# A fused attention and gated-FFN layer on one core: remainder weight rows in three loads, a slack on the q/k weights, and the last token block in two column pieces

## The chip, the cores and the metric

The kernel runs on one core of one Trainium2 chip. The metric is the device time of one execution in microseconds (us), the median of several. The core has a matrix engine (TensorE, PE in the profile), a vector engine (DVE), an activation engine (ScalarE, ACT), GpSimd (POOL) and SyncE (SP). Most DMAs are issued by SP, in program order; the scatter of q and k within SBUF is issued by POOL. Each engine runs its own instruction list in order, and waits on semaphores for the others.

## The reference

`x` has 2048 tokens of 576 features. It is layer-normalized; one branch is causal attention with 32 heads of 18 features and a window of 256 tokens, the other a gated FFN of width 4608. The result is `x` plus their gated product:

```python
xn = layernorm(x)
s  = attention(xn, wqkv, window=256) @ wo          # 32 heads of 18
h  = sigmoid(xn @ w_gate) * (xn @ w_up)            # 576 -> 4608
g  = silu(h @ w_down)                              # 4608 -> 576
return x + s * g                                   # bfloat16
```

## The kernel before

**Stages.** The tokens are taken in four stages of 512 (four blocks of 128). Each stage has a layernorm with transposes, v for its four blocks, five groups of q/k columns (128 columns each; the fifth is the rest of both), attention by eight groups of four heads, the product with wo, and the FFN: gate and up for 36 tiles of 128 hidden columns (`gate_up`, L828), the gating (`tail`, L844) and the down product (`down`, L885), last the gated sum and the store of each block (`build_final`, L909).

**Contraction of 576 as 64 + 4 x 128.** The 576 input features do not divide by 128. The first 64 weight rows, the *remainder rows*, have a tensor of their own, and the other 512 stand as four layers of 128 partitions. `load_nat` (L391) loads the 512, `load_rem` (L395) the 64. `pair` (L89) issues two matmuls of 64 rows each, one on each half of the array, and `turn` (L97) makes one *half* of a product: half 0 has ten matmuls and begins with the remainder rows, half 1 has eight and finishes the sum. So a product of gate and up of one tile is f10 (half 0, ten matmuls) and f11 (half 1, eight), and likewise qk0 and qk1, v0 and v1. For gate/up, the upper and lower partition halves of the remainder tensor `wgr` hold gate rows and up rows.

**Weights.** Gate and up are loaded in *groups* of two tiles, 256 KB from each of the two matrices, into a ring of four slots `wgs` (`weights`, L804); each of the four stages loads them again. The remainder rows of gate and up stay in `wgr` for all stages. Before the change they come in two loads of each matrix, set by `REM` (L57): the one beside group 0 covers groups 0 to 3, the one beside group 2 covers groups 4 to 17. A gate/up half of stage 0 waits for the loads of its own group and for those of the span that holds it. The q/k weights are `wqk` (two loads of 576 KB) and `wqkr` (two of 72 KB), those of v are `wv_sb` (576 KB) and `wvr` (two of 36 KB) (L423 to L426). The five copies L427 and L431 make the fifth q/k group's weights from `wqk` and `wqkr`.

**The order of the work is made by a planner.** The code first writes a graph of operations, each with an engine, an estimated duration, a priority (a smaller number goes first) and dependencies. `schedule` (L948) then goes through it as a list scheduler: at each step the operation that can start first by its own estimates is put at the end of its engine's list. A DMA is taken to end 2.5 us after its issue, or later if the bytes ahead of it need longer; a field `slack` adds to that end (used before the change for the loads of x, L387). `emit` writes the lists as they are, with waits on semaphores. So an estimate is no wait, it only moves places: on the chip each engine keeps its order, and an operation whose data is late holds up everything behind it on its engine.

**The start.** SP issues four loads of x, then group 0 and the first remainder span, groups 1 and 2, the second remainder span, group 3, the q/k weights, the v weights, then group 4 and so on. PE warms up on zeros (`NWARM`), transposes the normalized x, and does gate/up of tiles 0 to 2 (in two token halves each), then of tiles 3 and 4 except for the second half of tile 4. Behind that stand four halves of q/k, then v mixed with gate/up of tiles 4 to 6, then the first scores.

**The end.** The last stage's `build_final` differs from the others': ACT makes the tanh of each half of the columns, DVE multiplies the attention result with the PSUM value (L933, two halves of 288 columns), then combines (L938) and adds x (L943), and one DMA stores the block. The 576 output columns of a block lie in two PSUM banks of 288 (`halves`, L520); `down` does 36 hidden tiles in two turns over the partition halves, 72 pairs of matmuls of 288 columns.

Of the kernel before, what the change touches and what calls it, by code (L numbers as in the profile page):

```python
# [8 lines left out]
D = 576  # L9
# [79 lines left out]
def pair(eng, outs, lhs, rhs, start, stop, swap=0):  # L89
    res = None  # L90
    for i in range(2):
        t = i ^ swap
        res = eng.matmul(outs[i], lhs(ROWS[t], i), rhs(ROWS[t], i), start=start, stop=stop, tile_position=(64 * t, 0))  # L93
    return res
# [125 lines left out]
class Builder:  # L220
# [566 lines left out]
    def build_ffn(self, c):  # L787
# [16 lines left out]
        def weights(wg):  # L804
            sw, dw = self.r_w.produce()
            pr = 1 + wg if c == 0 and wg < 4 else 3
            fc = slice(wg * WG * P, (wg + 1) * WG * P)
            ds = [self.load_nat(self.wgs[:, sw, :, i, :], w[:, fc], f"dma:w:{c}:{wg}", ("w", sw, i), pr, [dw])
                  for i, w in enumerate((self.wg, self.wu))]
            if c == 0 and wg in REM:  # L810
                f8 = slice(REM[wg][0] * WG * P, REM[wg][1] * WG * P)
                self.op_wgr[wg] = self.load_rem(self.wgr[:, f8], (self.wg[:, f8], self.wu[:, f8]), f"dma:wgr:{wg}", ("wgr", wg), pr)
            if c == 0:
                ds += self.op_wgr[0 if wg < 4 else 2]
            slots[wg] = sw
            wops[wg] = ds

# [64 lines left out]

        new_last = [None] * NFG

        def down(i, h, swap, deps):  # L885
            cols = slice(i * P, (i + 1) * P)
            for q in range(NFG):
                def f(eng, q=q):
                    res = None
                    for ft in range(q * FG, (q + 1) * FG):  # L890
                        res = pair(eng, self.halves(h, 288), lambda r, t: self.hT[r, ft, cols],
                                   lambda r, t: self.wd_sb[r, ft, 288 * t:288 * t + 288],
                                   swap == 0 and ft == 0, swap == 1 and ft == NFT - 1, swap)
                    return res
                o = pe(FG * mm_ns(288), f, f"f2:{c * BPC + i}:{swap}:{q}",
                       [[hm[ft] for ft in range(q * FG, (q + 1) * FG)], self.op_wd[q], deps],
                       h if q == 0 and swap == 0 else None)
# [11 lines left out]
    def build_final(self, sb, h, f2):  # L909
        op = self.op  # L910
        sx, dx = self.r_xf.produce()
        st, dt_ = self.r_th.produce()
        rows = slice(sb * P, (sb + 1) * P)
        o_dx = self.dma(self.xf[:, sx, :], self.x[rows, :], P * D * 2, f"dma:xf:{sb}", ("xf", sx), deps=[dx, self.hm[8]], prio=6)
        t, xf, s_ = self.thf[:, st, :], self.xf[:, sx, :], self.s_attn[:, sb % BPC, :]

        def y2():
            return self.both(h, 288)

        def v2(a):  # L920
            return a.rearrange("p (t c) -> p t c", t=2)
        def f_th(e, a, b):
            return e.activation(v2(t)[:, a:b, :], y2()[:, a:b, :], ACTF.Tanh, scale=0.25)  # L923
        if sb < (NC - 1) * BPC:
            th = op("ACT", act_ns(D), lambda e: f_th(e, 0, 2), f"fth:{sb}", deps=[f2, dt_], prio=0)
            q1 = op("DVE", dve_ns(D), lambda e: e.scalar_tensor_tensor(v2(t), v2(t), 1.0, y2(), ALU.add, ALU.mult),  # L926
                    f"fq1:{sb}", deps=[th, f2], prio=0)
            q2 = op("DVE", dve_ns(D, 2.0), lambda e: e.tensor_tensor(t, t, s_, ALU.mult), f"fq2:{sb}",
                    deps=[q1, self.op_s[sb]], prio=2)
            h.release(q1)  # L930
        else:
            def f_w(e, a):
                return e.tensor_tensor(v2(s_)[:, a, :], v2(s_)[:, a, :], y2()[:, a, :], ALU.mult)  # L933
            th0 = op("ACT", act_ns(D // 2), lambda e: f_th(e, 0, 1), f"fth:{sb}:0", deps=[f2, dt_], prio=0)
            w1 = op("DVE", dve_ns(D // 2), lambda e: f_w(e, 1), f"fq1:{sb}:1", deps=[f2, self.op_s[sb]], prio=0)
            th1 = op("ACT", act_ns(D // 2), lambda e: f_th(e, 1, 2), f"fth:{sb}:1", deps=[w1, dt_], prio=0)
            w0 = op("DVE", dve_ns(D // 2), lambda e: f_w(e, 0), f"fq1:{sb}:0", deps=[th0, w1], prio=0)
            q2 = op("DVE", dve_ns(D), lambda e: e.scalar_tensor_tensor(t, t, 1.0, s_, ALU.add, ALU.mult), f"fq2:{sb}",  # L938
                    deps=[w0, th0, th1], prio=0)
            h.release(w0)  # L940
            h.release(th1)
        self.op_q2[sb] = q2
        q3 = op("DVE", dve_ns(D, 2.0), lambda e: e.tensor_tensor(xf, xf, t, ALU.add), f"fq3:{sb}", deps=[q2, o_dx], prio=2)  # L943
        self.r_th.release(st, q3)
        o = self.dma(self.out[rows, :], xf, P * D * 2, f"dma:out:{sb}", ("out", sx), deps=[q3], prio=2)
        self.r_xf.release(sx, o)

    def schedule(self):  # L948
        ENGS = ("PE", "ACT", "DVE", "POOL", "SP")
# [196 lines left out]
```

## Time and profile before

| | us |
|---|---|
| median of five runs | 593.98 (593.0 to 594.95) |
| the profiled execution | 594.95 |
| its span, from first to last instruction | 593.2 |
| PE busy | 575.6 |
| DVE busy | 345.8 |
| ACT busy | 274.5 |
| POOL busy | 176.3 |
| first gate/up matmul | 10.08 |
| first q/k matmul | 24.48 |
| first v matmul | 32.13 |
| first scores | 40.43 |
| last matmul ended | 588.20 |
| last DVE instruction ended | 590.50 |

Times inside the profile count from the start of the span. A line of the timeline has the start, the length, the engine, the source line, the operation with its output and input, and in brackets how long the engine sat idle before it and what released it. Matmuls are pipelined: the length of a merged line is what counts, not the mean of one. Where a line holds a DMA issue (SPq, POOLq), the length is that of issuing; the landing is given separately as the time from issue to landing. The two halves of a pair count as two matmuls.

### The profile page before, as it was taken

Reading aid. Unit: us, or ns where it says so; the run is one execution under the profiler, and the core shown is the slowest. Engines: PE = TensorE matmul, PEld = TensorE weight load, DVE = VectorE, ACT = ScalarE, POOL = GpSimd, SP = SyncE. Lnnn points to the kernel's source line nnn. Section 1 sums busy time; section 2 is a strip of 40 time slices with the busy share of each in tenths; the row PEclk is TensorE's granted clock in tenths of the full one; section 3 lists DMA queues with packets and bytes.
Section 4 is the critical chain, followed back from the end, with each engine's and each line's share of the span. In section 5 each row is a group of like instructions: output and inputs, shape, how many; then the busy total and the mean of one; then the engine's idle time right before and its main releaser. Section 6 shows DMA issues by size and latency. Waiting matters only on the chain.

```text
span 593.2 us, 21412 instructions
## 1 busy us (share of the span) xinstructions
PE 575.6 (97%) x9528; PEld 359.4 (61%) x9528; DVE 345.8 (58%) x837; ACT 274.5 (46%) x389; POOL 176.3 (30%) x286
## 2 busy tenths in 40 slices
PE   8798999999999999999999999999999999999996
PEld 7364455567788556455587775555447764444775
DVE  4268888855978783687866378867431133333122
ACT  2145667545556744587764356765230123233111
POOL 5362755108463440454620644340000000000000
PEclk9799999999999999999999999999999999999998
DMA  8936654642111442344300213333351113542010
GB/s 225 280 106 206 192 162 133 195 132 59 47 34 50 111 115 67 104 116 122 101 22 29 51 31 98 99 114 107 111 152 30 38 56 112 160 142 73 2 42 21
DMA packets 95724, 60.09 MB, mean 101 GB/s; under 512 B 7020, under 2 KB 94012, under 8 KB 95632
## 3 DMA queue, kind: packets, MB, share of 16 engines
q1 hardware_dynamic: 90512, 53.98, 31.9%
q0 software_dynamic: 5120, 4.74, 3.2%
q8 instruction: 75, 1.23, 0.9%
q14 instruction: 17, 0.14, 0.1%
HBM read 51.61 MB, written 2.36 MB: 91 GB/s over the span
## 4 chain that ended last, share of the span: by engine, by line
PE 83%; DVE 5%; DMA 3%; POOL 3%; SPq 3%; issue 2%; ACT 1%; DVEq 0%; POOLq 0%
PE ps L93 82%; POOL qk L249 3%; SPq L249 3%; DMA qk<-qd 2%; DVE qd L550 1%; DVE hT L849 1%; DMA wqkr<-in_A_wqkv_dram 1%; DVE pvs L728 1%; ACT tring L846 1%; PE ps L512 1%; DVE kx L627 1%; DVE v_aug L610 0%; ACT expr L662 0%; DVE expr L675 0%; DVE s_attn L933 0%
## 5 line engine op out<-in xcount | busy, mean ns | idle before, releaser
L93 PE MATMUL ps<-xnT,wgs 64*128 64x512 bf16 (+1 forms) x2352 | 287.2, 372 | 0.1
L662 ACT ACTIVATE expr<-ps 128x1024 bf16<-128x1024 f32 (+2 forms) x160 | 153.3, 983 | 63.0 <-PE ps L93 62.3
L93 PEld LDWEIGHTS ps<-xnT,wgs 64*128 64x128 bf16 x2352 | 112.6, 94 | 111.4 <-PE ps L93 0.9
L93 PE MATMUL ps<-wd_sb,hT 64*128 64x288 bf16 x2304 | 155.5, 283 | 0.0
L846 ACT ACTIVATE tring<-ps 128x512 bf16<-128x512 f32 x144 | 85.7, 598 | 135.7 <-PE ps L93 133.4
L849 DVE SCALAR_TENSOR_TENSOR hT<-tring,ps 128x512 bf16<-128x512 bf16 x144 | 98.1, 684 | 79.2 <-ACT tring L846 75.9
L93 PEld LDWEIGHTS ps<-wd_sb,hT 64*128 64x128 bf16 x2304 | 111.8, 94 | 27.9
L249 POOL DMA_DIRECT2D qk<-qd x160 | 81.8, 520 | 112.6 <-DVE qd L550 77.5
L675 DVE TENSOR_TENSOR expr<-expr,mask 128x256 bf16<-128x256 bf16 (+2 forms) x232 | 65.7, 307 | 39.8 <-ACT expr L662 38.7
L627 POOL TENSOR_SCALAR kx<-kprev,small 128x256 bf16<-128x256 bf16 x64 | 63.9, 1006 | 73.3 <-PE ps L93 73.0
L93 PE MATMUL ps<-xnT,wgr 64*128 64x512 bf16 (+1 forms) x294 | 55.5, 373 | 5.0 <-DVE hT L849 3.3
L93 PE MATMUL ps<-qk,kx 64*128 64x320 bf16 (+4 forms) x736 | 57.5, 251 | 0.7 <-DVE qd L550 0.3
L728 DVE TENSOR_REDUCE pvs<-ps 64x304 f32<-64x608 f32 x64 | 50.4, 787 | 8.6 <-PE ps L93 7.1
L93 PEld LDWEIGHTS ps<-qk,kx 64*128 64x128 bf16 x736 | 31.4, 94 | 23.8 <-DVE qd L550 1.2
L93 PEld LDWEIGHTS ps<-v_aug,expr 64*128 64x128 bf16 x2432 | 35.3, 93 | 7.4 <-DVE expr L675 2.2
L923 ACT ACTIVATE thf<-ps 128x576 bf16<-128x576 f32 (+1 forms) x20 | 11.1, 555 | 61.7 <-PE ps L93 61.4
L93 PE MATMUL ps<-v_aug,expr 64*128 64x19 bf16 (+1 forms) x2432 | 35.9, 170 | 0.9 <-DVE expr L675 0.8
L93 PE MATMUL ps<-xnT,wqk 64*128 64x512 bf16 x256 | 35.1, 399 | 0.0
L627 DVE TENSOR_SCALAR kx<-qk,small 128x512 bf16<-128x512 bf16 x64 | 23.6, 393 | 10.2 <-DMA qk<-qd 9.8
L550 DVE CAST qd<-ps 128x1024 bf16<-128x1024 f32 (+1 forms) x20 | 22.2, 1115 | 9.2 <-PE ps L93 8.9
L93 PEld LDWEIGHTS ps<-xnT,wgr 64*128 64x128 bf16 x294 | 14.6, 94 | 20.4 <-DVE hT L849 6.1
L926 DVE SCALAR_TENSOR_TENSOR thf<-thf,ps 128x576 bf16<-128x576 bf16 x12 | 9.0, 753 | 29.6 <-ACT thf L923 29.4
(65 smaller groups left out, 306.8 us busy)
## 6 DMA issues: line engine op xcount, KB each, us to landing
wgs<-in_B_w_gate_dram SPq DMA_DIRECT2D x72, 256.0 KB, 3.1
wgs<-in_B_w_up_dram SPq DMA_DIRECT2D x72, 256.0 KB, 3.5
wd_sb<-in_B_w_down_dram SPq DMA_DIRECT2D x9, 576.0 KB, 4.1
qk<-qd POOLq DMA_DIRECT2D x100, 36.0 KB, 1.9
xf<-in_A_x_dram SPq DMA_DIRECT2D x16, 144.0 KB, 2.3
out_dram<-xf SPq DMA_DIRECT2D x16, 144.0 KB, 1.8
xr<-in_A_x_dram SPq DMA_DIRECT2D x6, 288.0 KB, 3.3
wqk<-in_A_wqkv_dram SPq DMA_DIRECT2D x2, 576.0 KB, 11.0
```

Source lines behind the costliest of these rows:

```text
L93: res = eng.matmul(outs[i], lhs(ROWS[t], i), rhs(ROWS[t], i), start=start, stop=stop, tile_position=(64 * t, 0))
L249: o = self.op(eng, DMA_ISSUE_NS[eng], lambda e: e.dma_start(dst, src), name, deps, prio, nbytes=nbytes)
L512: res = eng.transpose(self.psb[:, o:o + 64], src(r, k * P), self.ident[r, :], tile_position=(64 * t, 0))
L550: return eng.tensor_copy(dst, self.both(h, n))
L627: return e.tensor_scalar(self.kx[:, sx, pos:pos + n_ // SW, t, :], src.rearrange("p (s k) -> p s k", k=SW), self.half[:, t:t + 1], None, A ...
L662: return eng.activation(self.expr[:, se, :, lo * SW:NT], self.both(h, NT)[:, :, lo * SW:NT], ACTF.Exp, scale=SM_SCALE)
L675: return eng.tensor_tensor(e_, e_, m_, ALU.mult)
L728: return eng.tensor_reduce(out[ROWS[i]], src, mybir.AxisListType.X, ALU.add)
L846: th = op("ACT", act_ns(NT), lambda e: e.activation(self.tring[:, st, :], bank(h, 0), ACTF.Tanh, scale=0.5), f"th:{c}:{ft}", deps=[pg, dt_ ...
L849: mu = op("DVE", dve_ns(NT), lambda e: e.scalar_tensor_tensor(self.hT[:, ft, :], self.tring[:, st, :], 1.0, bank(h, 1), ALU.add, ALU.mult) ...
L923: return e.activation(v2(t)[:, a:b, :], y2()[:, a:b, :], ACTF.Tanh, scale=0.25)
L926: q1 = op("DVE", dve_ns(D), lambda e: e.scalar_tensor_tensor(v2(t), v2(t), 1.0, y2(), ALU.add, ALU.mult), f"fq1:{sb}", deps=[th, f2], prio=0)
```

## The change

Three things are edited.

1. `REM` has three spans in place of two, each with a priority of its own: groups 0 and 1 beside group 0 (priority 1), groups 2 to 5 beside group 2 (priority 3), groups 6 to 17 beside group 3 (priority 7). Each span is a load from gate and one from up: 2 x 64 KB, 2 x 128 KB and 2 x 384 KB, in place of 2 x 128 KB and 2 x 448 KB. The group that needs a span waits for it.
2. The four loads of the q/k weights get a slack of 2500 ns in the planner.
3. In the last stage's last two blocks, the down product of block 15 is made in two column pieces: columns 0 to 383 (192 in each bank) and 384 to 575 (96 in each bank, `NTAIL`), the second one in a further PSUM hold from the attention's pool. On PE the first half of the small piece stands ahead of the last of the nine groups of hidden tiles of the large one (`NFG - 1`), and its second half comes last. `build_final` runs once for each piece; the store of the block stays one DMA and waits for both.

```diff
+NTAIL = 96
...
-REM = {0: (0, 4), 2: (4, 18)}
+REM = {0: (0, 2, 1), 2: (2, 6, 3), 3: (6, 18, 7)}
...
         self.op_wqk += self.load_rem(self.wqkr[:, :], (wq, wk), "dma:wqkr", ("wqkr",), 5)
+        for o in self.op_wqk:
+            o.slack = 2500.0
...
-                self.op_wgr[wg] = self.load_rem(self.wgr[:, f8], (self.wg[:, f8], self.wu[:, f8]), f"dma:wgr:{wg}", ("wgr", wg), pr)
+                self.op_wgr[wg] = self.load_rem(self.wgr[:, f8], (self.wg[:, f8], self.wu[:, f8]), f"dma:wgr:{wg}", ("wgr", wg), REM[wg][2])
             if c == 0:
-                ds += self.op_wgr[0 if wg < 4 else 2]
+                ds += self.op_wgr[0 if wg < 2 else 2 if wg < 6 else 3]
...
         for i in range(0, BPC, 2):
             hs = [self.pool_f.hold() for _ in range(2)]
-            lo = [down(i + j, hs[j], 0, []) for j in range(2)]
-            for j in range(2):
-                self.build_final(c * BPC + i + j, hs[j], down(i + j, hs[j], 1, [lo[j]]))
+            sb = c * BPC + i
+            if sb + 2 < NC * BPC:
+                lo = [down(i + j, hs[j], 0, []) for j in range(2)]
+                for j in range(2):
+                    self.build_final(sb + j, hs[j], down(i + j, hs[j], 1, [lo[j]]))
+                continue
+            ht = self.pool_s.hold()
+            na = D // 2 - NTAIL
+            lo = down(i, hs[0], 0, [])
+            la = down(i + 1, hs[1], 0, [], 0, na)
+            self.build_final(sb, hs[0], down(i, hs[0], 1, [lo]))
+            down(i + 1, hs[1], 1, [la], 0, na, range(NFG - 1))
+            lb = down(i + 1, ht, 0, [], 2 * na, NTAIL)
+            fa = down(i + 1, hs[1], 1, [la], 0, na, range(NFG - 1, NFG))
+            self.build_final(sb + 1, hs[1], fa, 0, na)
+            self.build_final(sb + 1, ht, down(i + 1, ht, 1, [lb], 2 * na, NTAIL), 2 * na, NTAIL)
...
-        q3 = op("DVE", dve_ns(D, 2.0), lambda e: e.tensor_tensor(xf, xf, t, ALU.add), f"fq3:{sb}", deps=[q2, o_dx], prio=2)
+        q3 = op("DVE", dve_ns(w, 2.0), lambda e: e.tensor_tensor(xf, xf, t, ALU.add), f"fq3:{nm}", deps=[q2, o_dx], prio=2)
...
+        if c0 == 0:
+            self.fq3 = []
+        self.fq3.append(q3)
+        if c0 + w == D:
+            o = self.dma(self.out[rows, :], self.xf[:, sx, :], P * D * 2, f"dma:out:{sb}", ("out", sx), deps=self.fq3, prio=2)
+            self.r_xf.release(sx, o)
```

`down` takes the first column `c0`, the width `n` in each bank and the groups of hidden tiles `qs` to do as arguments; `build_final` takes `c0` and `n`, and makes x's load and its buffers only for the piece that begins at column 0.

More of the change, by code (lines that the diff above doesn't have):

```diff
@@ L883, in build_ffn, with down @@
         new_last = [None] * NFG
-        def down(i, h, swap, deps):
+        def down(i, h, swap, deps, c0=0, n=288, qs=range(NFG)):
             cols = slice(i * P, (i + 1) * P)
-            for q in range(NFG):
+            for q in qs:
                 def f(eng, q=q):
@@ L890, in f @@
                     for ft in range(q * FG, (q + 1) * FG):
-                        res = pair(eng, self.halves(h, 288), lambda r, t: self.hT[r, ft, cols],
-                                   lambda r, t: self.wd_sb[r, ft, 288 * t:288 * t + 288],
+                        res = pair(eng, self.halves(h, n), lambda r, t: self.hT[r, ft, cols],
+                                   lambda r, t: self.wd_sb[r, ft, c0 + n * t:c0 + n * t + n],
                                    swap == 0 and ft == 0, swap == 1 and ft == NFT - 1, swap)
                     return res
-                o = pe(FG * mm_ns(288), f, f"f2:{c * BPC + i}:{swap}:{q}",
+                o = pe(FG * mm_ns(n), f, f"f2:{c * BPC + i}:{swap}:{q}",
                        [[hm[ft] for ft in range(q * FG, (q + 1) * FG)], self.op_wd[q], deps],
@@ L903, in build_ffn, with build_final @@
             hs = [self.pool_f.hold() for _ in range(2)]
-            lo = [down(i + j, hs[j], 0, []) for j in range(2)]
-            for j in range(2):
-                self.build_final(c * BPC + i + j, hs[j], down(i + j, hs[j], 1, [lo[j]]))
+            sb = c * BPC + i
[14 more added lines that the diff above has]
+            self.build_final(sb + 1, ht, down(i + 1, ht, 1, [lb], 2 * na, NTAIL), 2 * na, NTAIL)
         self.prev_f2_last = new_last
-    def build_final(self, sb, h, f2):
+    def build_final(self, sb, h, f2, c0=0, n=288):
         op = self.op
-        sx, dx = self.r_xf.produce()
-        st, dt_ = self.r_th.produce()
         rows = slice(sb * P, (sb + 1) * P)
-        o_dx = self.dma(self.xf[:, sx, :], self.x[rows, :], P * D * 2, f"dma:xf:{sb}", ("xf", sx), deps=[dx, self.hm[8]], prio=6)
-        t, xf, s_ = self.thf[:, st, :], self.xf[:, sx, :], self.s_attn[:, sb % BPC, :]
+        if c0 == 0:
+            sx, dx = self.r_xf.produce()
+            st, dt_ = self.r_th.produce()
+            o_dx = self.dma(self.xf[:, sx, :], self.x[rows, :], P * D * 2, f"dma:xf:{sb}", ("xf", sx), deps=[dx, self.hm[8]], prio=6)
+            self.fin = (sx, st, dt_, o_dx)
+        sx, st, dt_, o_dx = self.fin
+        w = 2 * n
+        cs = slice(c0, c0 + w)
+        t, xf, s_ = self.thf[:, st, cs], self.xf[:, sx, cs], self.s_attn[:, sb % BPC, cs]
+        nm = f"{sb}:{c0}"
         def y2():
-            return self.both(h, 288)
+            return self.both(h, n)
         def v2(a):
@@ L924, in build_final @@
         if sb < (NC - 1) * BPC:
[L925 to L928, printed above, removed]
+            th = op("ACT", act_ns(w), lambda e: f_th(e, 0, 2), f"fth:{nm}", deps=[f2, dt_], prio=0)
+            q1 = op("DVE", dve_ns(w), lambda e: e.scalar_tensor_tensor(v2(t), v2(t), 1.0, y2(), ALU.add, ALU.mult),
+                    f"fq1:{nm}", deps=[th, f2], prio=0)
+            q2 = op("DVE", dve_ns(w, 2.0), lambda e: e.tensor_tensor(t, t, s_, ALU.mult), f"fq2:{nm}",
                     deps=[q1, self.op_s[sb]], prio=2)
@@ L933, in f_w @@
                 return e.tensor_tensor(v2(s_)[:, a, :], v2(s_)[:, a, :], y2()[:, a, :], ALU.mult)
[L934 to L938, printed above, removed]
+            th0 = op("ACT", act_ns(n), lambda e: f_th(e, 0, 1), f"fth:{nm}:0", deps=[f2, dt_], prio=0)
+            w1 = op("DVE", dve_ns(n), lambda e: f_w(e, 1), f"fq1:{nm}:1", deps=[f2, self.op_s[sb]], prio=0)
+            th1 = op("ACT", act_ns(n), lambda e: f_th(e, 1, 2), f"fth:{nm}:1", deps=[w1, dt_], prio=0)
+            w0 = op("DVE", dve_ns(n), lambda e: f_w(e, 0), f"fq1:{nm}:0", deps=[th0, w1], prio=0)
+            q2 = op("DVE", dve_ns(w), lambda e: e.scalar_tensor_tensor(t, t, 1.0, s_, ALU.add, ALU.mult), f"fq2:{nm}",
                     deps=[w0, th0, th1], prio=0)
@@ L942, in build_final @@
         self.op_q2[sb] = q2
-        q3 = op("DVE", dve_ns(D, 2.0), lambda e: e.tensor_tensor(xf, xf, t, ALU.add), f"fq3:{sb}", deps=[q2, o_dx], prio=2)
+        q3 = op("DVE", dve_ns(w, 2.0), lambda e: e.tensor_tensor(xf, xf, t, ALU.add), f"fq3:{nm}", deps=[q2, o_dx], prio=2)
         self.r_th.release(st, q3)
-        o = self.dma(self.out[rows, :], xf, P * D * 2, f"dma:out:{sb}", ("out", sx), deps=[q3], prio=2)
-        self.r_xf.release(sx, o)
+        if c0 == 0:
+            self.fq3 = []
[3 more added lines that the diff above has]
+            self.r_xf.release(sx, o)
     def schedule(self):
```

## The prediction

> **What bounds the kernel now.** I read the busy shares first, then the chain that ended last in order of time, then PE's waits, then the two ends of the span in the timeline.
>
> ```profile
> span 593.2 us, 21412 instructions
> PE 575.6 (97%) x9528; PEld 359.4 (61%) x9528; DVE 345.8 (58%) x837; ACT 274.5 (46%) x389; POOL 176.3 (30%) x286
> ```
>
> PE (TensorE) is busy in all but 17.6 us. Both kernels do the same matmuls, except in the last block, so only PE's idle time, its clock and the work behind its last matmul can change. The chain tells where the idle time is (columns: start, length, what):
>
> ```profile
> 12.19 1.11 SPq L249
> ...
> 13.35 4.87 SPq L249
> 18.26 6.09 DMA wqkr<-in_A_wqkv_dram
> 24.35 0.14 issue
> 24.48 20.92 PE ps L93 x208
> ```
>
> PE's own list of waits has it as the longest one (total, times, longest):
>
> ```profile
> PE ps L93 <- DMA wqkr<-in_A_wqkv_dram: 4.4, 1, 4.4
> PE ps L93 <- DVE hT L849: 3.3, 8, 1.0
> PE ps L93 <- DMA wgr<-in_B_w_up_dram: 1.3, 1, 1.3
> ```
>
> So PE stood from 20.04 to 24.48 us for the q/k remainder rows, the last of a queue of loads. From 30.4 us to the last matmul (588.20) all waits together are 5.47 us (557.80 less 552.33 busy). Then the wait's second price, the clock (stretches; PE busy, PEld, DVE, ACT, POOL, then granted clock, DMA share, GB/s):
>
> ```profile
> 20.10:23.50 3.40, 0.00 (x0) 0.00 (x0) 0.00 (x0) 0.58 (x1) 0.00 (x0) 1.00 0.97 275
> 23.60:27.00 3.40, 2.52 (x13) 1.04 (x15) 1.79 (x7) 0.00 (x0) 0.00 (x0) 0.50 1.07 318
> 27.00:30.40 3.40, 3.40 (x18) 1.41 (x16) 0.00 (x0) 0.00 (x0) 0.00 (x0) 0.50 0.68 193
> 30.40:33.80 3.40, 3.40 (x38) 1.98 (x36) 3.04 (x3) 0.60 (x1) 1.65 (x3) 1.00 0.06 13
> ...
> 588.20:590.10 1.90, 0.00 (x0) 0.00 (x0) 1.72 (x4) 0.82 (x2) 0.00 (x0) 1.00 0.00 0
> 590.20:593.00 2.80, 0.00 (x0) 0.00 (x0) 0.30 (x1) 0.00 (x0) 0.00 (x0) 0.50 0.16 53
> ```
>
> From about 23.6 to 30.4 the clock is half, and PE works in it from 24.48: 5.92 us at half speed lose 2.96 us. The wait thus costs 4.44 + 2.96 = 7.4 us. The end (a DVE line, then ACT, then DVE):
>
> ```profile
> 588.20 1.01 DVE L933 TENSOR_TENSOR s_attn<-s_attn,ps 128x288 bf16<-128x288 bf16 x2 [2.11 <-PE ps L93]
> 588.20 0.90 ACT L923 ACTIVATE thf<-ps 128x288 bf16<-128x288 f32 x2 [3.51 <-PE ps L93]
> 589.25 0.76 DVE L938 SCALAR_TENSOR_TENSOR thf<-thf,s_attn 128x576 bf16<-128x576 bf16 x1
> 590.04 0.46 DVE L943 TENSOR_TENSOR xf<-xf,thf 128x576 bf16<-128x576 bf16 x1
> ```
>
> Behind the last matmul stand 2.30 us of DVE (588.20 to 590.50) and the store.
>
> **Part 1: the loads.** The built orders show SP's queue with the same loads in the same places up to wvr, only smaller: the first remainder pair is 2 x 64 KB instead of 2 x 128, the second 2 x 128 instead of 2 x 448. The 2 x 384 KB left over come directly behind wvr. So 768 KB are no longer ahead of the q/k and v weights. What are they worth? Landings in the trace (issue start plus time to landing): wgs group 0 at 3.1 + 4.7 = 7.8, the 128 KB pair at 4.25 + 5.7 = 9.95, wgs group 2 at 6.6 + 7.4 = 14.0, the 448 KB pair at 9.7 + 8.7 = 18.4. The 128 KB pair thus took 2.15 us of the queue, the 448 KB pair 4.4. By size of row: 448 to 128 saves 4.4 - 2.15 = 2.25; on the straight line through both pairs (3.5 us per 1000 KB) 128 to 64 saves 0.45; together 2.7. By bytes at each pair's own rate: 4.4 x 320/448 + 2.15 x 64/128 = 4.2. Bounds: 0, if only the number of packets counts, and 6.55, if both pairs cost nothing. I take the middle of the two row prices, 3.45 us.
>
> The Trainium skill ("DMA: Bandwidth & Descriptors", Rules for kernel authors) speaks against small loads: under 64 KB a transfer pays mostly overhead. If the 64 KB pair saved nothing by that rule, the saving would be about 3.0 instead of 3.45. No run here shows a 64 KB load.
>
> **Part 2: the slack moves the wait, it doesn't end it.** The slack only tells the planner that q/k come late, and PE's order changes: behind f11 of tile 3 (the second half of its gate/up product) stood the four q/k halves; now the v halves of token blocks 0 and 1 stand there (v0, v0, v1, v1), and q/k follow after all v. But wv and wvr are loaded *after* wqkr, and got no slack. The first v0 waits for both. In the trace wvr landed at 20.9 + 5.4 = 26.3, wqkr at 24.35. So the new wait ends at 26.33 - 3.45 + 0.13 (landing to matmul, as for wqkr) = 23.0, against 24.48: a gain of **1.5 us** (0.75 to 2.25 by the two row prices). Behind the waiting v0, in order, stand f11 of tile 4 and f10/f11 of tile 5, whose weights landed at 14.0; they can't pass. On DVE the five copies of the q/k rest (L427, L431) stand ahead of the product of tile 3; they waited 6.1 us until 24.47 and now get wqkr before PE resumes, so they hold nobody. The smaller first pair ends PE's 1.28 us wait at 10.08 by 0.45 to 1.07 us earlier; all of that becomes longer waiting at v0 and counts nothing. PE will stand from some 19.0 to 20.0 until 23.0.
>
> Who is late next? (a) q/k: from the first qd cast (30.63) to the end of the second kx (39.67 + 0.38 = 40.05) it took 9.4 us, of which 0.9 was v evictions in between. Between the product that this cast reads and the first scores the new order has two q/k and eight gate/up halves, 90 matmuls of 512 columns; 18 of them take 1.96 us (40.65 to 41.75 and 43.23 to 44.09), so 9.8 us. Cover is just enough; if it fails by 0.5 us, that is its price. (b) wgs of group 4 and the last remainder span: 768 KB more ahead of group 4, which landed at 21.6 + 5.4 = 27.0, so at about 27 to 28 now; PE needs it after 72 v matmuls (4.5 us) and ten halves (9.8 us) behind 23.0, at some 37 us. Hidden with 9 us to spare. Tiles from 12 on need the last span still later. SP only issues two more DMAs of about 0.6 us there. (c) The order of everything up to about 400 us is drawn anew on all engines. The 5.47 us of waits there belong to chains (scatter, kx, mask, pvs) that are the same in kind; I take no change, with 1.0 us each way.
>
> **Part 3: the clock.** Granted clock changes in this trace fall at 23.6, 30.4 and, 2 us behind the last matmul, at 590.1 to 590.2. The last is telling: PE was busy to 588.20 and was throttled after only 1.9 to 2.0 us of idling, while 1.28 us (8.8 to 10.08) brought nothing. So a wait of 3 to 4 us likely still costs a throttle. With the same phase it falls at 23.6, 0.6 us after PE resumes, and the next stretch of 3.4 us is busy throughout (in the old run it was busy for 2.52 only, and the clock stayed down for a second one). Half speed from 23.57 to 26.98 loses 1.7 us instead of 2.96: a gain of **1.25 us**. Bounds: 2.96 gained (no throttle), 0.45 lost (two full stretches).
>
> The Trainium skill ("TensorE: Matmul & The Clock Gate", Why this matters for your kernels) puts the limit at idle gaps of some 3 us, one whole idle window. By that rule a wait of 3.0 to 3.4 us would often go free and the gain be 2.96; the throttle 2 us behind the last matmul is against it, and I go by the row.
>
> **Part 4: the last block in two pieces.** Before, 72 pairs of 288 columns at 123.6 ns a pair (298 such matmuls in 18.42 us): 8.90 us. After, 72 pairs of 192 and 72 of 96. A pair of v_aug (19 or 38 columns) goes in 29.5 ns (35.9 us for 2432 matmuls), so weights don't hold 96 columns back; per column 0.417 ns plus 3.6 a pair gives 83.6 and 43.6 ns: 9.16 us, **0.26 more**; the last matmul is about 0.08 shorter. Only the 96-column piece stands behind it: DVE at 0.96 elements a ns less than the rows: 0.47 to 0.27 twice, 0.76 to 0.37, 0.46 to 0.26: 1.17 + 0.09 of gaps = 1.26 instead of 2.30. But DVE must first finish the 384-column piece: 0.37 + 0.37 + 0.57 + 0.36 and gaps, 1.85 us, while PE works only 36 x 43.6 = 1.57 on the rest. So 0.3 is given back: 1.04 - 0.3 - 0.18 = **0.5 us** gained (0.1 to 0.9). The store is one DMA as before.
>
> **Sum.** 1.5 + 1.25 + 0.5 = 3.25 us. The profiled execution took 594.95 us (span 593.2 and 1.75 around it), so 591.7; it is the slowest of the five, 0.97 above the median, and on the median of 593.98 the sum gives **590.7 us**.
>
> **Rivals.**
> *No throttle*: PE's wait is short enough or falls well between the stretches: 1.5 + 2.96 + 0.5 = 5.0, **589.0** (587.5 to 589.4). For it: the wait shrinks to about 3 us. Against: the throttle 2 us behind the end.
> *Nothing left*: the attention of stage 0 now starts later and is packed differently, and new waits in the middle, 3.3 us on the 5.47, eat the gain: 590.7 + 3.3 = **594.0** (592.8 to 595.2). For it: DVE is busy 20.38 of 22.8 us from 66.2 to 89.0. Against: gate/up work without any dependence on attention fills PE there.
> *Slower, the v wait*: packets, not bytes, set the landing (each span has 64 rows whatever its length). Then wvr still lands at 26.3, PE resumes at 26.46 and not 24.48, 1.98 us later, with the same clock loss: +1.98 - 0.5 = **595.5**. For it: the first 448 KB issue alone held SP 2.48 us, and the 128 KB pair cost 2.15 us, more per byte than the large one. Against: in the 448 KB pair bytes did cost. It decides where the smaller loads save less than 1.98 - 0.5 = 1.5 us and the clock loss stays.
>
> **How the numbers follow.** Forecast (589.4 to 592.8) 0.60, no throttle 0.17, nothing left 0.13, slower 0.10. A run of this kernel can tell about 0.2% (1.2 us) from no change. Faster by more: 0.60 + 0.17 = 0.77; same 0.13; slower 0.10. Range 587.5 to 593.4: both faster cases and the near part of "nothing left"; the row prices' best (2.25 + 2.96 + 0.9 = 6.1, 587.9) lies in it.
>
> **What would show it.** PE's longest wait names wvr or wv and ends at 22.2 to 23.8. The half clock lasts about 3.4 us of PE's work, or is not there. The second pair lands within 1.3 to 2.2 us behind wgs group 2. DVE ends about 1.6 us behind the last matmul. Waits from 30.4 us on sum to 4.5 to 6.5. I am wrong if v0 starts after 24.5, if the scores of head group 0 wait for q/k, or if those later waits pass 8 us.

## The result, and the profile after

The changed kernel takes **592.05 us** (median of 27 executions, 589.05 to 595.01), the kernel before 593.86 us (median of 50, 591.71 to 595.76) in the same comparison. The ratio is 0.9972 with a 95% interval of 0.9963 to 0.9981: 1.7 us faster by the ratio. The forecast was 590.7 us, 3.25 us faster. The sign is right and the time lies in the range; the gain is about half of what was forecast.

The profiled execution of the changed kernel took 593.62 us, 1.57 above its median; that of before was 0.97 above the median the forecast started from. The two spans are 593.2 and 591.9 us, 1.3 us apart. Its heading and busy shares (PEld is TensorE's loading of weights into the array, which overlaps PE):

```profile
span 591.9 us, 21714 instructions
PE 574.2 (97%) x9672; PEld 360.4 (61%) x9672; DVE 346.7 (59%) x841; ACT 274.6 (46%) x391; POOL 173.7 (29%) x286
```

The chain that ended last, in order of time (start, length, what):

```profile
15.77 9.47 DMA wvr<-in_A_wqkv_dram
25.38 12.70 PE ps L94 x125
38.10 1.24 DVE qd L553
39.63 3.73 POOL qk L250 x7
43.36 4.91 DMA qk<-qd
...
49.01 16.89 PE ps L94 x235
```

PE's waits (total, times, longest):

```profile
PE ps L94 <- DMA wvr<-in_A_wqkv_dram: 6.4, 1, 6.4
PE ps L94 <- DVE hT L852: 1.8, 7, 0.4
PE ps L94 <- DMA qk<-qd: 1.2, 1, 1.2
```

The wait for the q/k remainder rows is gone, and a longer one for those of v is there: PE stands from 18.99 to 25.38 us, where it stood from 20.04 to 24.48 before. It stops 1.05 us earlier, mostly because its first gate/up product waits 0.39 us for its smaller remainder pair, and not 1.28. It resumes 0.9 us later. A wait that is new on the chain is the scatter of q and k (a POOL DMA), 1.2 us ahead of the first scores.

The clock, and the traffic during the wait (stretch; busy time of PE, PEld, DVE, ACT, POOL; granted clock, DMA share, GB/s):

```profile
18.99:21.00 2.01, 0.00 (x0) 0.00 (x0) 0.00 (x0) 0.60 (x1) 1.00 (x2) 1.00 1.17 260
21.00:23.00 2.00, 0.00 (x0) 0.00 (x0) 1.67 (x7) 0.00 (x0) 0.00 (x0) 1.00 0.99 189
23.00:25.30 2.30, 0.00 (x0) 0.00 (x0) 0.11 (x1) 0.00 (x0) 0.00 (x0) 0.55 1.11 197
25.38:28.00 2.62, 2.62 (x24) 1.93 (x26) 0.00 (x0) 0.00 (x0) 0.00 (x0) 0.50 1.10 309
28.00:30.10 2.10, 2.10 (x20) 1.42 (x18) 1.07 (x3) 0.99 (x3) 0.00 (x0) 0.51 0.86 248
```

The clock is half from 23.2 to 30.0, two stretches as before. PE works in it from 25.38, 4.66 us, and loses half of that: 2.33 us, against 2.96 before. Note the last column: while wvr is on its way, the queues are busy (DMA share about 1), yet move only some 190 to 200 GB/s. In the kernel before it was 332 from 22 to 24 us, but 185 from 14 to 16 (rows in the last section).

The end of the timeline (start, length, engine, line, operation):

```profile
587.03 0.56 DVE L960 SCALAR_TENSOR_TENSOR thf<-thf,s_attn 128x384 bf16<-128x384 bf16 x1
587.62 0.36 DVE L965 TENSOR_TENSOR xf<-xf,thf 128x384 bf16<-128x384 bf16 x1
587.90 0.60 DVE L955 TENSOR_TENSOR s_attn<-s_attn,ps 128x96 bf16<-128x96 bf16 x2
588.54 0.36 DVE L960 SCALAR_TENSOR_TENSOR thf<-thf,s_attn 128x192 bf16<-128x192 bf16 x1
588.93 0.26 DVE L965 TENSOR_TENSOR xf<-xf,thf 128x192 bf16<-128x192 bf16 x1
```

The last matmul ends at 587.67. DVE is still at the wide piece then (to 587.98), so the narrow piece starts 0.23 us late, and DVE ends at 589.19: 1.5 us behind PE, against 2.30 before.

### The profile page after: what moved, and what is told of

Read it like the earlier page. It is cut to its first block, busy times and chain, and to the rows that moved or that the text cites. A ratio compares the mean times of both kernels' runs of the same rounds, so it can differ in the third digit from the quotient of the medians.

```text
span 591.9 us, 21714 instructions
## 1 busy us (share of the span) xinstructions
PE 574.2 (97%) x9672; PEld 360.4 (61%) x9672; DVE 346.7 (59%) x841; ACT 274.6 (46%) x391; POOL 173.7 (29%) x286
## 3 DMA queue, kind: packets, MB, share of 16 engines
q8 instruction: 76, 1.25, 0.9%
## 4 chain that ended last, share of the span: by engine, by line
PE 84%; DMA 4%; DVE 4%; POOL 2%; SPq 2%; issue 1%; ACT 1%; DVEq 0%; POOLq 0%
PE ps L94 83%; DMA qk<-qd 3%; POOL qk L250 2%; SPq L250 2%; DMA wvr<-in_A_wqkv_dram 2%; DVE qd L553 1%; DVE hT L852 1%; DVE pvs L731 1%; PE ps L515 1%; ACT tring L849 1%; DVE expr L678 0%; DVE kx L630 0%; DVE s_attn L955 0%; DVE thf L960 0%; DVE v_aug L613 0%
## 5 line engine op out<-in xcount | busy, mean ns | idle before, releaser
L94 PE MATMUL ps<-wd_sb,hT 64*128 64x288 bf16 (+2 forms) x2448 | 155.7, 276 | 0.0
L630 POOL TENSOR_SCALAR kx<-kprev,small 128x256 bf16<-128x256 bf16 x64 | 61.5, 971 | 75.1 <-PE ps L94 74.9
L678 DVE TENSOR_TENSOR expr<-expr,mask 128x256 bf16<-128x256 bf16 (+2 forms) x232 | 67.0, 312 | 27.6 <-ACT expr L665 25.5
L945 ACT ACTIVATE thf<-ps 128x576 bf16<-128x576 f32 (+3 forms) x22 | 11.4, 519 | 63.6 <-PE ps L94 63.1
L94 PE MATMUL ps<-xnT,wqk 64*128 64x512 bf16 x256 | 32.9, 376 | 0.0
L630 DVE TENSOR_SCALAR kx<-qk,small 128x512 bf16<-128x512 bf16 x64 | 22.2, 371 | 13.3 <-DMA qk<-qd 12.5
L612 ACT ACTIVATE v_aug<-ps 64x288 bf16<-64x288 f32 x32 | 13.1, 409 | 27.8 <-PE ps L94 27.2
```

What stands on the lines that cost most here:

```text
L612: return eng.activation(dst, src, ACTF.Copy)
L630: return e.tensor_scalar(self.kx[:, sx, pos:pos + n_ // SW, t, :], src.rearrange("p (s k) -> p s k", k=SW), self.half[:, t:t + 1], None, A ...
L678: return eng.tensor_tensor(e_, e_, m_, ALU.mult)
```

## The experiments

All ratios are against the kernel before, run beside the experiment on the same chip. The table gives what the theories are about: which weight wait PE has and when it ends, PE's idle time from 31 to 450 us (where attention is mixed in), and the number of half-clock stretches (3.4 us each) up to 450 us, from the profiled execution of each. Shorter waits for gate/up weights (up to 1.5 us, near 9 us) are not in the column of weight waits.

| kernel | median us | ratio (95%) | wait of PE for q/k or v weights, ends at | idle 31 to 450 | stretches |
|---|---|---|---|---|---|
| before | 593.86 | 1 | q/k 4.4, 24.48 | 5.4 | 2 |
| the change | 592.05 | 0.9972 (0.9963-0.9981) | v 6.4, 25.38 | 5.3 | 2 |
| e1 tail only | 593.18 | 0.9990 (0.9979-1.0001) | q/k 4.6, 24.52 | 5.0 | 2 |
| e2 slack only | 597.66 | 1.0058 (1.0045-1.0071) | v 4.9, 28.11 | 8.3 | 2 |
| e3 spans and tail | 597.3 | 1.0059 (1.0041-1.0077) | q/k 4.0, 21.26 | 9.0 | 2 |
| e4 PE kept busy | 591.8 | 0.9984 (0.9962-1.0006) | none | 6.9 | 0 |
| e5 the change again | 592.36 | 0.9982 (0.9969-0.9996) | v 7.3, 26.07 | 4.7 | 3 |
| e6 v loaded first | 586.72 | 0.9878 (0.9860-0.9897) | v 2.7, 18.38 | 2.9 | 1 |
| e7 v first, slack on v | 593.37 | 0.9987 (0.9971-1.0004) | none | 9.4 | 0 |
| e8 spans, tail, scatter late | 587.62 | 0.9896 (0.9879-0.9913) | q/k 4.0, 21.04 | 2.7 | 1 |
| e9 last span held back | 589.22 | 0.9926 (0.9903-0.9949) | v 2.9, 21.89 | 3.9 | 1 |
| e10 change, scatter late | 592.69 | 0.9983 (0.9967-0.9998) | v 5.4, 24.89 | 5.2 | 2 |
| e11 v first, all three slacks | **583.74** | 0.9835 (0.9812-0.9858) | none | 2.9 | 0 |
| e12 before, scatter late | 589.76 | 0.9930 (0.9912-0.9949) | q/k 4.0, 23.97 | 2.8 | 1 |

"Scatter late" is a slack of 2500 ns in the planner on POOL's scatters of q and k.

### One part of the change at a time

**e1: the two column pieces alone.** The edit is part 3 of the change, put into the kernel before.

```diff
+NTAIL = 96
...
-        def down(i, h, swap, deps):
+        def down(i, h, swap, deps, c0=0, n=288, qs=range(NFG)):
...
+            self.build_final(sb + 1, hs[1], fa, 0, na)
+            self.build_final(sb + 1, ht, down(i + 1, ht, 1, [lb], 2 * na, NTAIL), 2 * na, NTAIL)
```

> Only the last block's two column pieces; the loads and the slack are as before, and so is the order of the start. Theory A (the start decides, the tail is a small sure gain): the wait for wqkr is there again, about 4.4 us, with its stretch of half clock; DVE ends about 1.5 us behind the last matmul instead of 2.3, and the extra PE work is about 0.2 us: 0.5 to 0.8 us faster than before, ratio 0.9987 to 0.9992. Rival B (nearly all of the 1.8 us comes from the tail): 1.5 us or more faster, ratio 0.9975.

Measured: 0.57 us less in the median, the interval just reaching 1. The start is that of before (the q/k wait ends at 24.52). What follows: the pieces alone agree with the half microsecond forecast, though the interval spans from nothing to 1.2 us. They leave the wait for the weights as it was.

**e2: the slack alone.**

```diff
+        for o in self.op_wqk:
+            o.slack = 2500.0
```

> Only the slack on the q/k weights. The built order puts v ahead of q/k, and four more gate/up halves than in the full change (f10 of tile 5 and 6, f11 of tiles 3 and 4) ahead of v. Theory A: wvr lands at about 26.3 as before; PE reaches the first v at about 23.1 and waits some 3.3 us, so with 3.0 us more work done it stands as if it had resumed at 23.4 instead of 24.48: 1.0 us faster, and up to 1.3 more if the half clock is shorter: ratio 0.996 to 0.9985. Rival C (the new order loses in the middle what it gains at the start): the waits from 30 us on grow by over 1.5 us and the ratio is 1.000 or more.

Measured: 3.4 us *slower* (by the ratio). The wait moves to wvr as expected, but a new one appears in the middle. DVE's line, then PE's, from the timeline:

```profile
57.51 0.35 DVE L629 TENSOR_SCALAR kx<-qk,small 128x512 bf16<-128x512 bf16 x1 [3.22 <-DMA qk<-qd]
```

```profile
58.71 0.61 PE L93 MATMUL ps<-xnT,wgr 64*128 64x512 bf16 x2 [3.12 <-DVE hT L851]
```

```profile
58.40:61.70 3.30, 2.99 (x20) 1.33 (x22) 2.06 (x10) 0.42 (x1) 0.90 (x2) 0.50 0.00 1
61.80:64.00 2.20, 2.20 (x60) 1.29 (x58) 2.15 (x6) 1.78 (x4) 1.98 (x3) 1.00 0.15 34
```

Read them in this order. The kx product on DVE (with qk the input of the scores) needs the scattered q/k and stands there 3.22 us for the DMA. Behind it in DVE's list stands the hT product that frees the gate/up pair's PSUM, and PE waits for that 3.12 us, though gate/up itself needs nothing of the attention. The clock falls while PE still waits, and is half for one more stretch (58.33 to 61.75). This is the rival *nothing left* in its mechanism, at a larger price.

**e3: the spans and the pieces, without the slack.**

```diff
-        for o in self.op_wqk:
-            o.slack = 2500.0
```

> The full change without the slack: three spans and the two column pieces; the q/k halves stand first again, right behind f10 of tile 3, so the first two halves of cover are gone (f10 of tile 4, f11 of tile 3: 1.95 us). Theory A (the spans bring the q/k weights 3.3 us forward, and the slack then gives that back by putting v, which is loaded later, in front): wqkr lands at about 21.1, PE waits from 17.0 to 21.2, which counts like resuming at 23.15, where the full change resumed at 25.4: 1.5 to 2.5 us faster than the full change, about 590, ratio to before 0.993 to 0.995. Rival D (the slack's order is worth something for the rest, or the earlier q/k only meets a later wait for wvr): PE stands again at the first v by 1 us or more, and it is no faster than the full change, 592 or more.

Measured: 3.5 us slower. The q/k wait ends at 21.26, 3.2 us earlier than before: the smaller loads do bring these weights forward by about what was worked out. But near 80 us the mechanism of e2 is there again:

```profile
78.93 0.62 DVE L628 TENSOR_SCALAR kx<-qk,small 128x512 bf16<-128x512 bf16 x2 [3.08 <-DMA qk<-qd]
```

```profile
81.67 0.28 PE L94 MATMUL ps<-qk,kx 64*128 64x256 bf16 x2 [2.24 <-DVE pvs L729]
82.81 0.60 PE L94 MATMUL ps<-xnT,wgr 64*128 64x512 bf16 x2 [0.86 <-DVE hT L850]
```

In all, DVE's kx waits 20.8 us for scatters, against 9.8 before; the scatter that ends the 3.08 us was issued at 73.42 and landed 5.5 us later. The clock is half from 82.86 to 86.28.

What follows from e1 to e3: **the parts don't add.** The slack costs 3.4 us and the spans with the pieces 3.5, yet all three gain 1.7. Each edit lets the planner draw the order of DVE, POOL and PE anew, up to some 400 us, and the planner takes a scatter to land 2.5 us after its issue. Over the whole run the scatters take a median of 2.0 us in the kernel before, in the change and in e3 alike, but from 30 to 110 us the medians are 2.1, 3.3 and 2.8, and the longest of each run took 4.2, 5.0 and 5.9.

### The wait for the v weights

The step of the prediction in doubt here is "the new wait ends at 26.33 - 3.45 + 0.13 = 23.0". In the change's profile wvr's landing came at 25.24.

**e4: PE kept busy in the wait**, by 72 matmuls of 288 columns that read xnT and whose sum the first real v product overwrites. This is added work; nothing is left out.

```diff
+NKEEP = 36
...
+    v0 = next(o for o in b.prog["PE"] if o.name == "v0:0")
...
+        for _ in range(NKEEP):
+            res = pair(eng, b.halves(v0.acq, 288), lambda r, t: b.xnT[r, 0, 0, 0:P], lambda r, t: b.xnT[r, 0, 0, 0:288], True, True)
...
+    b.prog["PE"].insert(b.prog["PE"].index(v0), keep)
```

> The full change with 72 extra matmuls of 288 columns (4.4 us of PE) ahead of the first v, which read the normalized x and write a PSUM bank that v then overwrites; they don't wait for the v weights, everything else stands in the same order. Theory A: the wait for wvr ends where it did, about 25.4, but the clock stays full, so what the half clock cost is saved, 2.3 us in the profile shown: about 589.7 to 590.5, ratio 0.993 to 0.995. Rival E (the half clock costs nothing, since PE would only wait elsewhere later, for the scatter or for ACT): 592, ratio 0.997, and the waits from 30 us on grow by about 2 us.

Measured: a median of 591.8, about what the change gives, over a wide 590.02 to 598.43. The profiled execution (591.31 us) has the full clock throughout and no wait for v. In it wvr landed at 22.7, near the time forecast, and the waits from 31 to 450 are 6.9 us, where the change has 5.3. The granted clock recorded for the twelve executions goes from 0.993 to 1.000, so the added work did not keep it full in each; the eight at 0.998 or above have a median of 591.5. A gain of the throttle's size is not in these times, with one term (the middle) worse by 1.7 us. I call it inconclusive.

**e5: the change, unaltered**, to see how firm its landing is.

> The full change again, unaltered, for a second profile and more times on another occasion. Theory F (the landing of wvr is set by the slowest sixteenth of each transfer and differs from one execution to the next by some 2.5 us: 22.7 with PE kept busy, 24.7 without slack, 25.2 in the profile shown): it lands anywhere from 22.5 to 25.5, and the times spread over 4 us or more, around 592, where the kernel before spreads over 3. Rival G (25.2 is what this order of loads gives, and the kernel kept busy differed because its PE work differs): 25.0 to 25.5 again.

Measured: ratio 0.9982, its interval overlapping that of the first comparison. wvr landed at 25.94, the wait was 7.3 us, and the clock was half for three stretches (21.35 to 31.59). So the change's own order gave 25 to 26 us in two of two profiled executions. The same queue of loads in e4 and e10 gave 22.7 and 24.8, so the landing spreads over 22.7 to 25.9.

**e9: the last remainder span held back** until the v weights have landed. The dependency is added after the planner is done, so no order moves. SP issues in order, so every load behind that span is held too: group 4, a load of w_down and group 5, which SP issued from 17.7 us on in the change and from 23.0 us on here.

```diff
+    b.op_wgr[3][0].deps = b.op_wgr[3][0].deps + b.op_wv
```

> The full change, but the issue of the last remainder span (2 x 384 KB) waits until the v weights have landed; all lists stand in the same order, so every load behind it on SP is later too, by up to 7 us. Theory J (in the full change that span runs beside the last v loads: the queue moves only some 200 GB/s there and the packets of v take twice as long, so it pushes wvr from about 23 to 25 or 26): wvr lands at 21.8 to 23.5 and PE resumes 2 to 3 us earlier, 589 to 590.5, ratio 0.992 to 0.995. Rival K (the slowest sixteenth is slow by itself): wvr lands at 24.7 to 26 again, 592 or more, or a new wait for the weights of group 4 appears near 37 us.

Measured: 589.22 us, ratio 0.9926: about 2.7 us less than the change (0.9926 / 0.9972 = 0.9954). From the timeline, and from the traffic in the same stretches:

```profile
21.89 0.35 PE L94 MATMUL ps<-wvr,xnT 64*128 64x288 bf16 x2 [2.92 <-DMA wvr<-in_A_wqkv_dram]
```

```profile
18.00:20.00 2.00, 0.98 (x10) 0.25 (x6) 0.00 (x0) 0.60 (x1) 1.95 (x3) 1.00 0.95 257
20.00:22.00 2.00, 0.11 (x2) 0.14 (x4) 1.70 (x7) 0.00 (x0) 0.00 (x0) 1.00 0.18 59
```

The traffic runs out by 20 to 22 us (59 GB/s; in the change 203, at a DMA share of 1.09), wvr lands at 21.76, and PE resumes 3.5 us earlier than in the change. The order of the work is the same: the loads **behind** wvr were what made it late. Whether it was the span's 768 KB alone or also the loads behind them, this run doesn't separate. PE has no later wait for the held span or the groups behind it. The waits from 31 to 450 us are smaller too (3.9 and 5.3 us), so part of the 2.7 us may lie there; and the profiled execution, 587.87 us, is the fastest of the six.

**e6: v loaded ahead of q/k** (priorities of the two swapped).

```diff
-... "dma:wqk", ("wqk", i), 5) ... "dma:wqkr", ("wqkr",), 5)
+... "dma:wqk", ("wqk", i), 6) ... "dma:wqkr", ("wqkr",), 6)
-... "dma:wv", ("wv",), 6)] ... "dma:wvr", ("wvr",), 6)
+... "dma:wv", ("wv",), 5)] ... "dma:wvr", ("wvr",), 5)
```

> The full change with the v weights loaded ahead of the q/k weights (priorities 5 and 6 exchanged). The planner then puts the first v behind f11 of tile 1, at about 15 us. Theory A (PE's wait at the start is for whichever weights the new order needs first, so loading those first ends it): wvr lands at 17 to 18.5, PE waits 2 to 3 us there instead of 6.4 and doesn't wait for q/k (wqkr at 23 to 25, needed at about 26): 3 to 4 us less idle and perhaps the half clock gone: 586 to 589, ratio 0.987 to 0.992. Rival C (another order, another long wait for the scatter of q and k in the middle, with its half clock): 592 or more.

Measured: 586.72 us. The planner now puts the first v product earlier on PE as well. The load that PE needs first is loaded first, and only 2.7 us of wait are left:

```profile
18.38 0.30 PE L94 MATMUL ps<-wvr,xnT 64*128 64x288 bf16 x2 [2.71 <-DMA wvr<-in_A_wqkv_dram]
```

Still the clock falls, from 19.69 to 23.11. The idle time in the middle is also smaller, 2.9 against 5.3, so not all of the 5 us is the load's.

### The waits in the middle

**e8: e3 with the scatters called late.** If the planner's belief that a scatter lands in 2.5 us is what puts kx too early in DVE's list, a slack on the scatters alone must cure e3.

```diff
                 o = self.dma(dst, src, n_ * 2 * NT * 2 // len(moves), f"dma:sp:{c}:{u}:{w}:{gi}", ("qk", par, gi),
                              deps=[ev, war, self.op_qz], prio=1, eng="POOL")
+                o.slack = 2500.0
```

> The change without the slack on the q/k weights, but with 2500 ns of slack on the scatters of q and k in the planner, so that it puts the kx products and the scores that need them later. Without the slack on the scatters that kernel had a wait of 3.1 us in two pieces near 80 us, for a kx that stood in DVE's queue until a scatter had landed 5.5 us after its issue, and half clock for 3.4 us behind it. Theory C (this wait and its clock are what made it slower): both go, DVE waits less for the scatter, and it is 3 to 5 us faster than without, 592.5 to 594.3, ratio 0.998 to 1.001. Rival H (the earlier q/k costs by itself, through cover lost at the start): 596 or more, ratio 1.004 or more.

Measured: 587.62 us, 9.7 less than e3, more than expected. DVE's list of waits has no row left of kx waiting for a scatter, the waits from 31 to 450 are 2.7 us and not 9.0, and the only half-clock stretch is the one behind the q/k wait (21.31 to 24.72).

**e12: the same slack in the kernel before**, nothing else.

```diff
+                o.slack = 2500.0
```

> The kernel before with 2500 ns of slack on the scatters and nothing else. Theory C: the wait for wqkr and its half clock are as before (4.4 us), the waits from 31 to 450 us fall from 5.4 to about 2.7: 590.5 to 591.5, ratio 0.9945 to 0.996. Rival L (in the kernel before no wait of the scatter is long, so there is nothing to win): 593 to 594.

Measured: 589.76 us, ratio 0.9930. One line in the kernel *before* is worth more than twice the whole change. DVE's wait for the scatters, before and with the slack:

```profile
DVE kx L627 <- DMA qk<-qd: 9.8, 11, 1.8
```

```profile
DVE kx L628 <- DMA qk<-qd: 2.6, 1, 2.6
```

PE's waits in the middle go from 5.4 to 2.8 us; in the profiled execution the clock is also half for one stretch, 25.21 to 28.63, and not for two. The slack is not a truer estimate but a cautious one: it makes the planner count on 5.0 us, where the scatters of the kernel before took a median of 2.0 and at most 4.2.

**e10: the same slack in the changed kernel**, by the same line.

```diff
+                o.slack = 2500.0
```

> The full change with 2500 ns of slack on the scatters of q and k. Theory C (the planner takes the scatters to land too soon, so its order has waits of kx in the middle, whose size each change of the start draws anew): the waits from 31 to 450 us, 5.3 us in the full change, fall to about 2.7 as they did when the same slack was added to the kernel without slack on q/k; wvr lands at 25 to 26 as in the full change: 589 to 590.5, ratio 0.992 to 0.995. Rival L (only that one long wait of 3 us with its half clock was to be had): 591.5 to 592.5.

Measured: 592.69 us, ratio 0.9983: no gain over the change. DVE's kx waits only 1.7 us for scatters here, against 12.5 in the change, so the slack did what it says. But PE's idle time in the middle stays, 5.2 us, 2.95 of it between 60 and 110 us; the longest row after the weight wait is now hT (3.8 us in 9 waits over the whole span). So the theory "the scatters are the waits" holds for e3 and for the kernel before, not for every order.

### Taken together

**e7: v loaded first, the slack on v too.** The priorities are those of e6, and:

```diff
+        for o in self.op_wv:
+            o.slack = 2500.0
```

> The same with a slack of 2500 ns on the v weights too: f10 of tiles 3 and 4 now stand ahead of the first v, which PE reaches at about 18. Theory A: wvr has landed by then or nearly so, no wait over 1 us at the start and no half clock there; q/k are needed at about 25.4 and wqkr lands at 23 to 25: 584 to 587, ratio 0.983 to 0.988. Rival C: an order planned on late loads misfits in the middle, one wait of 3 us or more with its half clock comes back: 589 or more.

Measured: 593.37 us. No wait for v or q/k weights is left and the clock is full throughout the profiled execution; all of it is given back in the middle:

```profile
PE ps L94 <- DVE hT L854: 6.4, 15, 1.4
...
PE ps L94 <- DVE kx L632: 1.3, 1, 1.3
...
PE ps L94 <- DMA qk<-qd: 0.8, 1, 0.8
```

**e11: e7 with the scatters called late as well.**

```diff
+                o.slack = 2500.0
```

> The v weights loaded first, slack on v and q/k, and 2500 ns of slack on the scatters. Without the last this kernel had no wait for weights and a full clock throughout, but 9.4 us of short waits from 31 to 450 us (hT, scatter) and 593.4 us. Theory C: these fall to 3 or 4 us, so 586.5 to 588.5, ratio 0.988 to 0.991, the fastest or equal to the kernel with v loaded first and no slack on v (586.7). Rival M (more gate/up ahead of the attention is what makes the later waits, whatever the scatter's estimate): 591 or more.

Measured: **583.74 us**, ratio 0.9835 (0.9812 to 0.9858): the best of all, 9.8 us below before, and below what was expected. Its rows show both ends cured, the start and the middle (PE's busy time is the second number after the stretch):

```profile
0.00:31.00 31.00, 28.02 (x460) 20.87 (x462) 16.98 (x56) 10.35 (x19) 13.68 (x22) 1.00 0.94 251
31.00:60.00 29.00, 28.69 (x400) 15.05 (x397) 20.43 (x55) 14.72 (x22) 14.57 (x25) 1.00 0.82 235
60.00:110.00 50.00, 48.79 (x828) 25.74 (x824) 42.53 (x113) 31.93 (x47) 24.54 (x41) 1.00 0.56 158
```

PE is idle for 2.98 us of the first 31 (before: 7.17), the granted clock is full, and from 31 to 110 another 1.5 us are idle.

## Why the prediction was right in sign and wrong in size

**The chain and the wait: right.** The slack moved the wait and did not end it; PE's longest wait names wvr, and the v halves stand in front.

**Part 2, "the new wait ends at 26.33 - 3.45 + 0.13 = 23.0": this step failed.** A gain of 1.5 us was forecast, and PE resumes 0.9 us *later*. The saving of 3.45 us was about right where it was made: the up load of wgs group 3 lands 4.7 us earlier (15.2 for 19.9) and wqkr 3.3 us earlier (21.06 for 24.35). It was wrong to carry it on to wvr, which landed only 1.1 us earlier (25.24). I had counted the 2 x 384 KB as gone because they stand behind wvr in SP's list. They and the loads behind them run *beside* it, at some 200 GB/s, and e9 shows it: with these held back, wvr lands at 21.76. Two of my signs of being wrong were met: v0 starts after 24.5, and the first scores wait for q/k. (In part 1, the middle of the two row prices without the 64 KB pair is 2.7 us, not 3.0; nothing rests on it.)

The Trainium skill ("DMA: Bandwidth & Descriptors", Two DMAs through the same engine are not ordered) says that descriptors on one queue start in order but are pipelined, and that nothing orders them across the 16 engines; wvr's landing 3.5 us later with loads behind it (25.24) than without (21.76) agrees with it.

**Part 3, a gain of 1.25 us by the clock: half right.** 2.96 - 2.33 = 0.63 us was gained. The wait did cost a throttle, as the row at the end of the span suggested, and *no throttle* didn't come. But with 6.4 us of wait, and not 3 to 4, the clock fell at 23.2, 2.2 us before PE resumed, and stayed down for a second stretch. That follows from the failed step; where the wait was 2.9 us (e9) or 2.7 (e6), one stretch was left, as part 3 had it. "With the same phase" had no ground: the fall came at 23.57 before, at 23.2 in the change and at 21.35 in the same kernel again (e5), so how much of a stretch PE spends working is in part luck.

**Part 4, 0.5 us: right as far as can be told.** e1 measured 0.57, with an interval from nothing to 1.2. In the profile DVE ends 0.8 us less behind PE; against that, the last stage's down products on PE take 35.62 us and not 35.44, 0.18 more where 0.26 was worked out.

**(a) "Cover is just enough": it failed** by 1.2 us (the scores wait for the scatter), the forecast price was 0.5. **(c) the middle: right in the sum, by luck in the parts.** 5.47 us were forecast unchanged, and 5.3 measured (from 30.1 us to the last matmul). The slack alone and the spans with the pieces each made it 3 to 4 us worse (8.3 and 9.0), and my reason, "chains that are the same in kind", does not exclude that. The rival *nothing left* had the right mechanism and should have had more than 0.13.

**The sum.** By the profile: +1.06 of idle time in the first 31 us, -0.16 from there to 450, -0.63 of clock, +0.18 and -0.78 at the end: -0.3 us. The spans differ by -1.3 and the medians by -1.8. So 1 us or more of the gain stays open: PE's last matmul comes some 1 us earlier than these terms say. The last down products already begin 0.68 us earlier (552.04 for 552.72), so it lies ahead of them, in time that the profile counts as busy. Why executions of the change spread more (589 to 595 us) is open in part too. The landing of wvr differs (25.24, 25.94), and so does the clock: of the 27 executions and the profiled one, the eight with a granted clock of 0.995 or above have a median of 590.9 us, the other twenty 592.6. But 3.5 to 4 us of spread are left within each group.

## What to carry to other kernels

Loads that stand behind a waited-for load are not out of its way: hold them back until it has landed, and load first what the order of the work needs first. Where a planner draws the order, one cautious estimate (here: a scatter taken to land after 5 us, though most took 2) can be worth more than the loads themselves, and its effect must be measured in each order, since the same line gave 9.7 us (e8), 9.6 (e11 against e7), 4 (e12) and 0 (e10). When a part of a change is judged, look at the whole order that it moves: three edits that cost 3.4 and 3.5 us apart gained 1.7 together.

## What the runs showed of the hardware that I had not expected

**The queues can be busy at 200 GB/s.** In the 4 us ahead of wvr's landing the DMA share was about 1 and the traffic 189 to 197 GB/s, while the v weights and the long remainder rows (64 partitions) were under way. The kernel before shows the same low rate earlier, from 14 to 16 us, while its own long rows (2 x 448 KB) were under way, and more after they had landed (18.4), 215 at a share of 0.90 from 20 to 22 us, then 332:

```profile
14.00:16.00 2.00, 2.00 (x42) 1.79 (x38) 0.00 (x0) 0.53 (x1) 1.94 (x3) 1.00 1.03 185
...
22.00:24.00 2.00, 0.00 (x0) 0.00 (x0) 0.00 (x0) 0.00 (x0) 0.00 (x0) 0.89 1.03 332
```

That the long rows cause the low rate fits both traces, but it wasn't measured by itself.

**The clock falls after less idling than I thought, by a grid.** In e6 a wait of 2.71 us was enough, in e9 one of 2.92, in e2 one of 3.12 and in e3 two of 2.24 and 0.86 with two matmuls between them. The half-clock stretches of all these traces last 3.42, 6.83 or 10.24 us; in the kernel before they lie on one grid of 3.41 us: from 23.57 to 30.40 it is two steps, and from there to 590.18 it is 164 steps of 3.413. The fall can come after the wait: 1.31 us after it in e6 (18.38, 19.69) and 1.24 in e12 (23.97, 25.21). In the grid step that ended with the fall PE had stood for only 2.1 and 2.2 us of the 3.41. The Trainium skill ("TensorE: Matmul & The Clock Gate", Why this matters for your kernels) gives gaps of about 3 us, one idle window, as the limit; the 2.71 us of e6 are below it, fill no whole step of the grid, and still cost a stretch.
